# Sink values of two head pairs as two row tiles of the tensor engine, in a fused attention and channel-mix kernel with a written order

## The chip, the cores and the metric

The kernel runs on one core of one Trainium2 chip. The metric is the device time of one execution in microseconds. The engines are named as in the profile: PE (TensorE, with PEld for its weight loads), DVE (VectorE), ACT (ScalarE), POOL (GpSimd) and SP (SyncE, which issues nearly all DMAs). PSUM is the memory into which PE writes its products; it has eight banks.

## The reference

Two layers run one after another. The first is attention over a sliding window of 128 positions with 4 sink positions that every query sees, for 4 batches, 8 heads, 768 positions and a head size of 64. The second is a channel mix with a model width of 512 and a hidden width of 1024.

```python
# attention
scores = scale * np.matmul(q, k.transpose(0, 1, 3, 2))
keep = is_sink | in_window          # pos < 4, or 0 <= query - key < 128
scores = np.where(keep, scores, -1e9)
a = np.exp(scores - max); a = a / (sum(a) + 1e-9)
x = np.matmul(a, v)                 # heads side by side: 512 columns
# channel mix
xk = mu_k * x + (1 - mu_k) * x_prev      # x_prev: the row before
xr = mu_r * x + (1 - mu_r) * x_prev
k = np.maximum(xk @ w_k, 0)
out = sigmoid(xr @ w_r) * (k * k @ w_v)
```

## The kernel before

The work is cut into 12 units, u = 3 * batch + T, of 256 positions each. In the code T is 0, 1 or 2, and g and j count the two blocks of 128 positions in a unit. Four head pairs (c = 0 to 3) make up the eight heads.

`prepare` casts q, k and v of a unit from float32 to bfloat16 (tiles qb, kb, vb) and turns q and k round to qt and kt, with the head's 64 columns of two heads on the 128 partitions. For the early units PE transposes them through a bank, and ACT or DVE copies the bank out (L624). k from unit 4 and q from unit 8 are transposed by a DMA on SP's queue (L603) instead. vb has a column of ones behind each head's 64 columns, so that the sum of the weights comes out as a 65th column. For each batch, `prepare` also makes ksink (the keys of the 4 sinks, by POOL, L655) and vsink (the sinks' values). vsink has the values of every head in rows of its own and zeros elsewhere: hmask keeps, for head h, four rows.

`attend` makes, for units with T > 0, the scores of the sinks (sink_scores, L678: one matmul per head pair, 32 columns of PE each, written to 32 partitions of a bank). ACT takes their exponent into es, which holds all heads: 128 rows and 256 queries. Then come, two head pairs at a time, the scores of the window (scores, L701), which run as two row tiles of 64 partitions, one head each, into the two tiles called sc of two banks each. ACT takes the exponent (L737, e), DVE multiplies the mask in (L751), PE makes the values (values), DVE the reciprocal (L788) and the product x (L791).

In values, one bank takes a head pair: two blocks of queries, two heads, 65 columns. For units with T > 0, each block of queries starts with one sink matmul over all 128 rows (L763), which gives both heads at once, since rows of other head pairs meet zeros of vsink. Then come four matmuls of 65 columns (L775).

`mix` turns x round by PE (L814) and copies it to xt (L823, ACT or DVE). DVE makes the difference td (L841) and the eight mixtures xk and xr (L852). `ffn` makes the hidden layer (L902), the relu (L912 by ACT or L916 by DVE), its square kk (L924, DVE), the gate (L933, with ACT's tanh at L939), the last product (L951, L872) and the output ob (L960, DVE), which SP stores.

Nothing is scheduled at run time. Every operation is put down with `P.op`; its number is its place in that list. ORDER gives each engine's line of operations by number, and each engine works its line through in order. CHOICE says, for some numbers, which engine takes an operation that several could take (casts, copies out of a bank, relus). The planner, `Plan.schedule`, follows the lines with estimated costs, gives out buffers from pools (`take`, held until the last operation that has it under `hold`), and puts filler matmuls (P.fill, L971) into PE's line where it finds PE idle in the first 22 us of its estimate. There are two tiles sc and four single banks, which the sinks' scores, the values, the transposes and all of `ffn` share. `mode` on a PE operation says which partition of the array it uses: 0 is the full array, 1 is row tiles, 2 is the sinks' scores, 4 the transpose of mu.

Of the kernel before, what the change touches and what calls it, by code (L numbers as in the profile page):

```python
# [18 lines left out]
    79: "ACT", 82: "ACT", 83: "ACT", 85: "ACT", 87: "ACT", 89: "DVE", 94: "DVE", 95:  # L19
    "DVE", 97: "DVE", 101: "DVE", 102: "DVE", 128: "DVE", 134: "DVE", 136: "DVE", 137:  # L20
    "DVE", 140: "ACT", 141: "DVE", 150: "DVE", 191: "DVE", 192: "ACT", 193: "ACT", 218:
    "DVE", 265: "DVE", 273: "DVE", 278: "DVE", 305: "DVE", 343: "DVE", 346: "DVE", 348:
    "DVE", 352: "ACT", 354: "DVE", 361: "DVE", 423: "DVE", 429: "ACT", 430: "ACT", 499:
    "DVE", 501: "DVE", 504: "DVE", 507: "DVE", 508: "ACT", 520: "DVE", 586: "ACT", 587:
    "ACT", 654: "DVE", 658: "DVE", 660: "DVE", 663: "DVE", 672: "DVE", 736: "DVE", 738:
    "ACT", 739: "DVE", 744: "DVE", 751: "DVE", 815: "DVE", 816: "ACT", 825: "DVE", 885:
    "DVE", 887: "DVE", 891: "ACT", 892: "ACT", 1003: "DVE",
# [24 lines left out]
        90, 93, 106, 96, 99, 104, 117, 77, 109, 114, 132, 138, 142, 129, 125, 120, 156,  # L52
        135, 158, 149, 184, 190, 169, 236, 208, 209, 212, 213, 220, 221, 161, 166, 172,
        177, 216, 194, 181, 201, 217, 187, 238, 291, 299, 292, 295, 300, 303, 249, 304,
        226, 296, 241, 246, 307, 224, 228, 277, 232, 229, 252, 261, 233, 267, 257, 311,
        264, 284, 270, 312, 319, 344, 309, 315, 330, 316, 349, 367, 375, 368, 376, 322,
        371, 395, 327, 372, 333, 338, 397, 275, 353, 379, 360, 380, 383, 408, 385, 387,
        422, 388, 445, 453, 446, 454, 400, 427, 405, 475, 411, 416, 391, 431, 392, 457,
        438, 458, 449, 473, 486, 450, 463, 526, 530, 527, 531, 500, 538, 461, 505, 539,
        469, 510, 470, 554, 478, 483, 534, 494, 489, 535, 512, 565, 557, 465, 579, 466,  # L60
        542, 519, 544, 562, 550, 584, 573, 551, 588, 546, 568, 632, 602, 547, 603, 606,
        614, 607, 595, 630, 643, 615, 620, 610, 618, 611, 640, 635, 678, 682, 679, 683,
        664, 646, 690, 706, 708, 686, 651, 687, 691, 626, 671, 719, 711, 622, 627, 694,
        623, 761, 757, 765, 758, 762, 766, 722, 696, 741, 727, 716, 775, 785, 702, 750,
        769, 743, 770, 796, 703, 788, 793, 698, 773, 699, 817, 777, 781, 778, 782, 835,
        831, 839, 832, 836, 799, 840, 859, 861, 843, 804, 847, 844, 824, 855, 849, 869,
        864, 872, 856, 907, 915, 908, 851, 916, 852, 880, 875, 911, 893, 912, 919, 900,
        920, 935, 937, 923, 925, 931, 948, 932, 973, 940, 974, 981, 945, 982, 951, 977,
        959, 978, 956, 985, 927, 966, 986, 928, 991, 989, 1001, 1009, 1005, 1002, 1013,
        1006, 1014, 1010, 993, 1021, 997, 994, 998, 1017, 1019, 1022, 1029, 1025, 1030,  # L70
        1026,
    ),
    "DVE": (
        69, 70, 89, 94, 95, 101, 97, 108, 102, 113, 110, 115, 111, 78, 137, 105, 116, 119,
        128, 124, 144, 126, 121, 134, 122, 127, 136, 150, 145, 151, 152, 146, 153, 191,
        147, 160, 148, 165, 80, 81, 154, 171, 141, 176, 162, 163, 167, 173, 168, 178, 174,
        179, 155, 196, 197, 203, 198, 205, 204, 211, 218, 199, 223, 206, 207, 84, 240,
        245, 305, 200, 86, 242, 306, 243, 247, 215, 248, 256, 219, 88, 278, 251, 294, 298,
        279, 230, 253, 302, 254, 234, 258, 259, 280, 265, 343, 286, 348, 281, 282, 287,
        289, 346, 321, 288, 313, 326, 317, 273, 337, 290, 323, 332, 324, 328, 283, 329,  # L80
        334, 339, 335, 340, 370, 354, 276, 374, 355, 361, 358, 362, 382, 356, 378, 364,
        357, 363, 423, 389, 399, 404, 410, 401, 415, 406, 402, 366, 412, 417, 407, 418,
        413, 359, 365, 448, 433, 393, 434, 440, 435, 442, 441, 456, 460, 499, 482, 477,
        504, 452, 529, 501, 488, 507, 436, 493, 511, 437, 471, 479, 480, 484, 444, 485,
        495, 556, 496, 490, 541, 491, 443, 537, 558, 572, 514, 559, 561, 533, 467, 515,
        520, 563, 521, 564, 517, 567, 574, 522, 575, 516, 523, 590, 552, 569, 591, 570,
        518, 525, 548, 524, 654, 634, 593, 639, 597, 660, 599, 658, 592, 598, 605, 645,
        636, 641, 637, 642, 650, 600, 617, 601, 613, 666, 647, 594, 609, 648, 652, 710,
        653, 669, 663, 667, 693, 668, 712, 672, 673, 675, 674, 676, 713, 628, 681, 624,
        670, 736, 721, 715, 726, 723, 724, 677, 685, 728, 729, 689, 760, 717, 742, 718,  # L90
        764, 792, 787, 751, 768, 739, 744, 789, 790, 794, 745, 704, 795, 746, 772, 752,
        748, 803, 747, 754, 753, 755, 700, 819, 779, 783, 798, 820, 749, 822, 834, 800,
        756, 801, 838, 805, 806, 815, 863, 842, 868, 825, 826, 821, 846, 827, 865, 828,
        866, 870, 885, 857, 823, 879, 887, 871, 829, 874, 853, 876, 881, 882, 877, 910,
        830, 918, 895, 898, 914, 902, 896, 922, 903, 939, 904, 944, 897, 933, 950, 941,
        942, 946, 947, 952, 955, 953, 905, 957, 958, 899, 961, 962, 906, 968, 976, 963,
        970, 969, 929, 980, 964, 972, 988, 984, 1003, 965, 1004, 1008, 971, 1012, 1016,
        995, 999, 1023, 1031, 1027,
    ),
    "ACT": (  # L100
        67, 68, 92, 91, 98, 112, 107, 100, 118, 131, 123, 133, 143, 139, 130, 183, 189,
        164, 159, 185, 79, 157, 175, 170, 82, 140, 210, 222, 237, 214, 180, 186, 195, 202,
        182, 192, 188, 244, 239, 293, 83, 301, 193, 255, 227, 250, 85, 297, 308, 87, 225,
        260, 266, 262, 263, 269, 268, 285, 271, 341, 325, 320, 345, 310, 336, 331, 350,
        369, 377, 396, 373, 419, 403, 398, 381, 421, 384, 424, 409, 386, 414, 352, 426,
        447, 455, 428, 481, 476, 432, 497, 439, 429, 502, 459, 451, 474, 487, 464, 528,
        532, 430, 492, 462, 506, 540, 560, 555, 508, 578, 536, 513, 571, 576, 580, 581,
# [188 lines left out]
def kernel(  # L296
# [14 lines left out]
    nc = tc.nc  # L311
    B, H, S, D = q.shape
# [5 lines left out]
    NP = H // 2  # L318
# [7 lines left out]
    P = Plan()  # L326
# [188 lines left out]
    def make_hmask():  # L515
        for a in range(2):
            m = hmask[:, a::2, :]
            keep(m, -4 * a, [[-32, NP], [0, D + 1]], 1, m)
            keep(m, 3 + 4 * a, [[32, NP], [0, D + 1]], -1, m)
# [504 lines left out]
```

## Time and profile before

| what | number |
| --- | --- |
| runs | 170.07, 171.16, 172.91 us; median 171.16 |
| profiled execution | span 172.5 us (the page gives no other time for it) |
| PE busy | 160.6 us (93%) |
| DVE busy | 153.6 us (89%) |
| ACT busy | 129.2 us (75%) |
| POOL busy | 13.4 us (8%) |
| L902 on PE | 384 matmuls, 52.0 us |
| L763 on PE, the sink values | 64 matmuls of 130 columns, 12.4 us |
| L775 on PE, the other values | 352 matmuls of 65 columns, 18.9 us |
| casts of vb on POOL | 3, 2.6 us |
| L971 on PE, fillers | 24 matmuls, 8.8 us |

Busy time is the time in which at least one instruction of the engine runs. Matmuls overlap each other, and their ends are modelled, so that PE's busy time is longer than what its matmuls need one behind another. A line such as L902 is a line of the kernel before. The symbol "<-" behind an idle time names what ended it.

### The profile page before, as it was taken

The page shows a single profiled execution, that of the slowest core. Times are in us where ns is not written, and L with a number is a line of the kernel's source. Part 1 is how long each engine was busy: PE and PEld are TensorE (multiplying, and loading weights), DVE is VectorE, ACT ScalarE, POOL GpSimd, SP SyncE. Part 2 cuts the span into 40 slices and gives each one's busy share as a digit, 9 for nine tenths or more (in the row PEclk, how much of TensorE's full clock was granted, in tenths as well). Part 3 has the DMA queues.
Part 4 walks back from the last instruction along what each step waited for, and adds up shares of the span by engine and source line. Part 5 has one row for each costly group of instructions (what it writes and reads, how often), then busy time and mean ns, then how long its engine had stood idle before and what let it go on. Part 6 is the DMA issues. An engine that isn't in the chain of part 4 may idle for free.

```text
span 172.5 us, 4178 instructions
## 1 busy us (share of the span) xinstructions
PE 160.6 (93%) x1588; PEld 106.3 (62%) x1605; DVE 153.6 (89%) x404; ACT 129.2 (75%) x208; POOL 13.4 (8%) x32
## 2 busy tenths in 40 slices
PE   7986869799999999999999999999999997999992
PEld 2444547675647667777567786756476773777551
DVE  6279895999999999999999999999999999699542
ACT  2488895999898999898979987865838958853320
POOL 7330000000010010050000200120000000000000
PEclk9999678999999999999999999999999999999999
DMA  4999999999156969999679489869969857102033
GB/s 144 243 302 365 291 254 353 380 298 229 26 139 157 287 124 240 197 257 289 163 170 226 96 212 243 159 170 212 240 149 256 213 111 211 61 4 113 11 122 122
DMA packets 81763, 33.82 MB, mean 196 GB/s; under 512 B 63688, under 2 KB 76240, under 8 KB 81744
## 3 DMA queue, kind: packets, MB, share of 16 engines
q1 hardware_dynamic: 81728, 33.56, 78.0%
q8 instruction: 12, 0.20, 0.6%
q14 instruction: 7, 0.06, 0.1%
q10 hardware_dynamic: 16, 0.00, 0.0%
HBM read 24.12 MB, written 6.29 MB: 176 GB/s over the span
## 4 chain that ended last, share of the span: by engine, by line
PE 82%; DVE 10%; DMA 3%; ACT 2%; issue 1%; DVEq 0%; ACTq 0%
PE bank L951 23%; PE bank L902 23%; PE bank L933 12%; PE sc L701 6%; PE bank L775 6%; PE bank L971 4%; PE bank L814 3%; DMA kt<-kb 3%; DVE e L751 2%; PE bank L616 2%; PE bank L763 2%; DVE xk L852 2%; ACT rl L912 1%; ACT e L737 1%; DVE x L791 1%
## 5 line engine op out<-in xcount | busy, mean ns | idle before, releaser
L902 PE MATMUL bank<-xk,wk_sb 128*128 128x256 bf16 x384 | 52.0, 278 | 1.6 <-DVE wk_sb L558 1.3
L737 ACT ACTIVATE e<-sc 128x1024 bf16<-128x1024 f32 (+1 forms) x48 | 44.5, 964 | 4.0 <-PE sc L701 4.0
L951 PE MATMUL bank<-wv_h,kk 128*128 128x512 bf16 x174 | 44.9, 379 | 0.7 <-issue 0.3
L902 PEld LDWEIGHTS <-wk_sb 128*128 128x128 bf16 x384 | 36.1, 100 | 10.2 <-DVE wk_sb L558 1.6
L912 ACT ACTIVATE rl<-bank 128x512 bf16<-128x512 f32 x45 | 26.2, 608 | 12.2 <-PE bank L902 9.6
L751 DVE TENSOR_TENSOR e<-e,mask 128x1024 bf16<-128x1024 bf16 (+1 forms) x48 | 30.0, 637 | 0.7 <-ACT e L737 0.7
L951 PEld LDWEIGHTS <-kk 128*128 128x128 bf16 x184 | 16.7, 98 | 15.8 <-issue 0.7
L933 PE MATMUL bank<-wr_sb,xr 128*128 128x512 bf16 x89 | 23.6, 379 | 0.3
L852 DVE SCALAR_TENSOR_TENSOR xk<-td,mu_all,xt 128x256 bf16<-128x256 bf16 x48 | 22.4, 491 | 0.1
L852 DVE SCALAR_TENSOR_TENSOR xr<-td,mu_all,xt 128x256 bf16<-128x256 bf16 x48 | 22.4, 476 | 0.0
L939 ACT ACTIVATE th<-bank 128x512 f32<-128x512 f32 x24 | 14.7, 618 | 7.8 <-PE bank L933 7.7
L960 DVE SCALAR_TENSOR_TENSOR ob<-th,bank 128x512 f32<-128x512 f32 x23 | 15.6, 680 | 5.6 <-ACT th L939 3.5
L791 DVE TENSOR_TENSOR x<-bank,rec 128x256 bf16<-128x256 f32 x48 | 19.4, 416 | 0.4
L924 DVE TENSOR_TENSOR kk<-rl 128x512 bf16<-128x512 bf16 x48 | 19.4, 415 | 0.1
L775 PE MATMUL bank<-vb,e 128*128 128x65 bf16 x352 | 18.9, 193 | 0.2
L775 PEld LDWEIGHTS <-e 128*128 128x128 bf16 x352 | 16.4, 98 | 3.0 <-DVE e L751 0.7
L701 PE MATMUL sc<-qt,kt 64*128 64x128 bf16 (+1 forms) x256 | 15.0, 246 | 1.7 <-DMA kt<-kb 0.9
L701 PEld LDWEIGHTS <-kt 64*128 64x128 bf16 x256 | 9.4, 97 | 7.9 <-issue 3.4
L933 PEld LDWEIGHTS <-xr 128*128 128x128 bf16 x96 | 8.9, 98 | 8.5 <-issue 0.3
L763 PE MATMUL bank<-vsink,es 128*128 128x130 bf16 x64 | 12.4, 220 | 0.4 <-ACT rl L912 0.3
L823 ACT COPY xt<-bank 128x512 bf16<-128x512 bf16 x15 | 8.8, 586 | 5.3 <-PE bank L814 5.1
L788 DVE RECIPROCAL rec<-bank 128x4 f32<-128x4 f32 x48 | 8.0, 174 | 3.2 <-ACT rl L912 1.8
(67 smaller groups left out, 166.5 us busy)
## 6 DMA issues: line engine op xcount, KB each, us to landing
vs<-in_v_dram SPq DMA_DIRECT2D x24, 256.0 KB, 3.9
out_dram<-ob SPq DMA_DIRECT2D x23, 256.0 KB, 3.2
ks<-in_k_dram SPq DMA_DIRECT2D x18, 256.0 KB, 4.7
qs<-in_q_dram SPq DMA_DIRECT2D x7, 512.0 KB, 9.5
qs<-in_q_dram SPq DMA_DIRECT2D x10, 256.0 KB, 5.4
w<-in_moe_w_k_dram SPq DMA_DIRECT2D x2, 1024.0 KB, 9.2
w<-in_moe_w_v_dram SPq DMA_DIRECT2D x2, 1024.0 KB, 9.9
ks<-in_k_dram SPq DMA_DIRECT2D x3, 512.0 KB, 8.0
```

The lines of the kernel that those rows point to most:

```text
L701: nc.tensor.matmul(out=sc[:, a, o0:o1], lhsT=lhs[rows], rhs=rhs[rows], start=u not in BIAS, stop=True, skip_group_check=u in BIAS)
L737: nc.scalar.activation(out=buf[ek][:, :, lo:], in_=buf[sck][:, :, lo:], func=AF.Exp, scale=scale)
L751: nc.vector.tensor_tensor(out=at, in0=at, in1=m, op=ALU.mult)
L763: nc.tensor.matmul(out=o[:, g, :, :], lhsT=buf["es", u][:, 128 * g:128 * g + 128], rhs=vsink[b % 2][:, 2 * c:2 * c + 2, :], start=True, st ...
L775: nc.tensor.matmul(out=o[:, g, a, :], lhsT=e[:, a, e0:e0 + 128], rhs=rhs, start=(T == 0 and i == 0), stop=(i == len(blocks) - 1), skip_gro ...
L791: P.op("DVE", dve(256), lambda ok=ok, rk=rk, c=c: nc.vector.tensor_tensor(out=buf["x", u][:, :, 128 * c:128 * c + 128].rearrange("p g (a d ...
L852: nc.vector.scalar_tensor_tensor(out=buf[key][:, c0 + i, :], in0=buf[tk][:, i, :], scalar=mu[w][:, c0 + i:c0 + i + 1], in1=xt[:, c0 + i, t ...
L902: nc.tensor.matmul(out=ps[:, i, :], lhsT=wk_sb[:, c, 128 * f:128 * f + 128], rhs=xk[:, c, :], start=(c == 0), stop=(c == NC - 1), skip_gro ...
L912: nc.scalar.activation(out=buf[rk], in_=buf[psk].rearrange("p (i t) -> p i t", i=2), func=AF.Relu)
L924: P.op("DVE", dve(512, 0.52), lambda f2=f2, rk=rk: nc.vector.tensor_tensor(out=buf["kk", u][:, 2 * f2:2 * f2 + 2, :], in0=buf[rk], in1=buf ...
L933: nc.tensor.matmul(out=buf[psk], lhsT=buf["xr", u][:, c, 128 * g:128 * g + 128], rhs=wr_sb[:, c, :], start=(c == 0), stop=(c == NC - 1))
L951: nc.tensor.matmul(out=buf[psk], rhs=wv_h[:, f, :], lhsT=buf["kk", u][:, f, 128 * g:128 * g + 128], start=(f == 0), stop=(f == NF - 1))
```

## The change

The sink rows are laid out anew. Head pair c had the rows from 32c; now it has those from 32 * (c // 2) + 64 * (c % 2). So head pairs 0 and 2 lie in the lower 64 rows, 1 and 3 in the upper. sink_scores writes to these rows, and hmask is made to fit.

The sink matmuls leave values and become an operation of their own, sink_values, once for two head pairs. It takes two banks. For each block of queries it issues two matmuls, one over the lower 64 rows into one bank, one over the upper 64 into the other. The values operations of the two head pairs find their bank taken and add to it. There are 64 such matmuls as before, in 16 operations, and the numbers of all later operations shift.

The tables ORDER and CHOICE are new. In CHOICE POOL has 18 entries, where it had none; POOL's line grows from 13 to 30 operations. It makes 11 casts of qb, 6 of kb, 2 of vb and one of wk_sb; before, it made 3 of vb. On DVE there are fewer casts of kb and qb (6 instead of 16), copies of xt (4 instead of 9), copies of qt (3 instead of 5) and casts of wk_sb (1 instead of 2), and more relus (6 instead of 3), casts of vb (9 instead of 8) and of wv_h (3 instead of 2). On ACT relus go from 45 to 42, casts of wv_h from 2 to 1, of kb from 16 to 14 and of qb from 16 to 11; copies of qt go from 11 to 13 and of xt from 15 to 20. PE's line has 42 fillers instead of 24. SP's line is the same up to the weights, and mixes loads, transposes and stores anew behind them; LOADS and the transposes by DMA stay as they were.

```diff
 CHOICE = {
-    79: "ACT", 82: "ACT", 83: "ACT", 85: "ACT", 87: "ACT", 89: "DVE", 94: "DVE", 95:
+    79: "ACT", 81: "POOL", 82: "ACT", 83: "ACT", 87: "ACT", 91: "DVE", 92: "POOL", 94:
...
 ORDER = {
...
     "POOL": (
-        72, 71, 73, 74, 75, 103, 76, 274, 272, 351, 509, 662, 740,
+        71, 74, 92, 72, 73, 75, 76, 131, 103, 81, 182, 270, 267, 345, 273, 352, 350,
+        278, 425, 430, 432, 356, 512, 436, 591, 517, 670, 825, 752, 903,
     ),
...
     def make_hmask():
         for a in range(2):
-            m = hmask[:, a::2, :]
-            keep(m, -4 * a, [[-32, NP], [0, D + 1]], 1, m)
-            keep(m, 3 + 4 * a, [[32, NP], [0, D + 1]], -1, m)
+            m = hmask[:, a::2, :].rearrange("p (i k) d -> p i k d", k=2)
+            keep(m, -4 * a, [[-32, 2], [-64, 2], [0, D + 1]], 1, m)
+            keep(m, 3 + 4 * a, [[32, 2], [64, 2], [0, D + 1]], -1, m)
...
             def sink_scores():
                 for c in range(NP):
-                    nc.tensor.matmul(out=buf[psk][32 * c:32 * c + 32, 0:256],
+                    r0 = 32 * (c // 2) + 64 * (c % 2)
+                    nc.tensor.matmul(out=buf[psk][r0:r0 + 32, 0:256],
...
+                if T > 0:
+
+                    def sink_values(cs=cs):
+                        for g in range(2):
+                            for r, i in enumerate(cs):
+                                rows = slice(64 * r, 64 * r + 64)
+                                o = buf["o", u, i][:, 130 * g:130 * g + 130]
+                                nc.tensor.matmul(
+                                    out=o.rearrange("p (a d) -> p a d", a=2),
+                                    lhsT=buf["es", u][rows, 128 * g:128 * g + 128],
+                                    rhs=vsink[b % 2][rows, 2 * i:2 * i + 2, :],
+                                    start=(g == 0), stop=False, skip_group_check=True)
+
+                    P.op("PE", 114.0, sink_values, r + 1, lag=PE_LAG, mode=1,
+                         take=[("bank", ("o", u, i)) for i in cs], hold=[("es", u)],
+                         writes=[("os", u, i) for i in cs], reads=[("es", u), ("vsink", b % 2)])
...
                 for g in range(2):
-                    if T > 0:
-                        nc.tensor.matmul(out=o[:, g, :, :],
-                                         lhsT=buf["es", u][:, 128 * g:128 * g + 128],
-                                         rhs=vsink[b % 2][:, 2 * c:2 * c + 2, :],
-                                         start=True, stop=False, skip_group_check=True)
...
-            P.op("PE", 358.0 if T else 180.0, values, r + 1, lag=PE_LAG, take=[("bank", ok)],
-                 hold=[ek, ("vb", u)] + ([("vb", u - 1), ("es", u)] if T else []), writes=[ok],
+            P.op("PE", 232.0 if T else 176.0, values, r + 1, lag=PE_LAG,
+                 take=[] if T else [("bank", ok)],
+                 hold=[ek, ("vb", u)] + ([("vb", u - 1), ok] if T else []), writes=[ok],
```

## The prediction

> **What bounds the kernel now.** I read the page's first two parts first, then the busy time by stretch, because an average hides a start-up and a tail.
>
> ```profile
> PE 160.6 (93%) x1588; PEld 106.3 (62%) x1605; DVE 153.6 (89%) x404; ACT 129.2 (75%) x208; POOL 13.4 (8%) x32
> ...
> PEclk9999678999999999999999999999999999999999
> ```
>
> The digits of PEclk are the granted clock in 40 slices: it sinks once, from 17 to 28 us. By stretch:
>
> ```profile
> 20.70:24.10 3.40, 1.55 (x12) 0.90 (x12) 3.40 (x8) 3.40 (x5) 0.00 (x0) 1.00 1.00 239
> 24.10:27.50 3.40, 3.13 (x15) 2.26 (x16) 2.74 (x6) 1.52 (x3) 0.00 (x0) 0.50 1.00 308
> 30.70:153.40 122.70, 119.74 (x1268) 81.36 (x1282) 119.86 (x315) 102.84 (x167) 7.46 (x9) 1.00 0.82 192
> 153.40:172.50 19.10, 15.85 (x101) 9.64 (x101) 11.55 (x27) 5.44 (x10) 0.00 (x0) 1.00 0.22 83
> ```
>
> The columns of a stretch are its length, then the busy time of PE, PEld, DVE, ACT and POOL, then the granted PE clock. There are three stages. The ramp lasts until 30.7 us, where DVE writes the last x of unit 1. The middle lasts to 153.4, where DVE writes the last x of unit 11. The tail runs to the end. In the middle PE and DVE both show about 98%. DVE's figure is real: its instructions start when the one before lets go, and only 2.8 of 122.7 us are idle. PE's is flattered, since a matmul is counted until its modelled end, long after the next one started (L902: mean 278 ns, but the chain of waits takes 1.75 us for 16, 109 ns each). So I take DVE as the bound of the middle, although the chain puts 82% on PE, and cost the middle on both engines. The tail is PE alone (L902, L951, L933, L872 without a break).
>
> **The change on PE.** In the timeline of PE one sink matmul (L763) starts 0.055 to 0.06 us ahead of the next matmul. The 64 of them take 64 x 0.056 = 3.6 us. As pairs in two row groups and two banks they should behave as the scores' pairs do (L701): twelve of those, six pairs, fit in 0.55 us together with the change of mode. So 32 pairs x 0.056 = 1.8 us remain, and 1.8 us are removed. What speaks against it is what a change of mode costs. In the chain of waits (start, us, what):
>
> ```profile
> 90.19 0.55 PE sc L701 x12
> 90.74 0.54 PE bank L902 x4
> 91.28 0.86 PE bank L951 x4
> 92.15 1.75 PE bank L902 x16
> ```
>
> Four L902 matmuls take 1.75 / 4 = 0.44 us, but 0.54 just behind the scores: leaving the tiled mode costs 0.10. The scores' own columns (two pairs of 256, four of 128) come to 0.45 of their 0.55, so entering costs 0.10 too. Counted along the two written PE orders by the operations' modes, there are 59 changes of mode before and 79 after: 20 x 0.10 = 2.0 us added. PE's account is -1.8 + 2.0 = +0.2 us: nothing is won there. I put it at zero on the path, because PE has cover in the middle. If PE were the bound after all, it would cost 0.2.
>
> The new operation takes two of the four single banks before its first matmul and keeps both until DVE has written the pairs' x. Behind a late bank all of PE's line waits. The trace has only small waits of this kind (L616 on DVE's x, 0.7 us, once), so I bound it by 0 and 1 us and take 0, as the nearest row is one wait in a whole run. The permuted rows in sink_scores and hmask change no count or size.
>
> **The change on DVE and POOL.** The new tables move more than the title says. Counted from the orders, between the last x of unit 1 and the last x of unit 11, DVE loses 6 copies of xt, 5 casts to qb, 2 copies of qt and 1 square, and gains 1 weight cast and 1 relu. DVE overlaps neighbours, so I price by start to start:
>
> ```profile
> 115.03 0.75 DVE L924 TENSOR_TENSOR kk<-rl 128x512 bf16<-128x512 bf16 x2
> 125.93 1.28 DVE L960 SCALAR_TENSOR_TENSOR ob<-th,bank 128x512 f32<-128x512 f32 x2
> 71.41 1.26 DVE L852 SCALAR_TENSOR_TENSOR xk<-td,mu_all,xt 128x256 bf16<-128x256 bf16 x3
> ...
> 47.71 0.61 POOL L638 CAST vb<-vs 128x512 bf16<-128x512 f32 x1
> ...
> 47.26 0.73 DVE L624 COPY qt<-bank 128x512 bf16<-128x512 bf16 x1
> 47.89 0.71 DVE L590 CAST qb<-qs 128x512 bf16<-128x512 f32 x1
> 48.86 0.41 DVE L590 CAST qb<-qs 128x512 bf16<-128x512 f32 x1
> ...
> 61.59 0.81 POOL L638 CAST vb<-vs 128x512 bf16<-128x512 f32 x1 [13.28 <-DMA vs<-in_v_dram]
> 61.45 1.62 DVE L852 SCALAR_TENSOR_TENSOR xk<-td,mu_all,xt 128x256 bf16<-128x256 bf16 x3
> ...
> 73.76 2.44 POOL L655 COPY ksink<-kt 64x16 bf16<-64x16 bf16 x2 [11.36 <-DMA kt<-kb]
> ```
>
> Two squares of about 0.415 each fit in 0.75, so a short operation costs 0.335 us; two L960 of 0.68 in 1.28 make a long one 0.60; a copy of qt takes 0.63 (47.26 to 47.89). Removed: 12 x 0.335 + 2 x 0.63 = 5.3. Added: 2 x 0.60 = 1.2. Net -4.1 us in the middle.
>
> POOL gets the casts. It makes 16 casts in the middle after, 3 before. The three old ones show what one does to DVE: the cast of qb at 47.89 took 0.71 where the next took 0.41 (+0.30); three L852 at 61.45 took 1.62 where three undisturbed ones took 1.26 (+0.36); at 97.07, beside a cast from 96.49 on, two took 1.23 where two others took 0.87 (+0.36). So a cast on POOL holds DVE up for about 0.34 us, as long as DVE itself would need for it. The 13 more cost 13 x 0.34 = +4.4. The bounds are 0, where DVE reads PSUM meanwhile (the ksink copies under the qt copy at 47.26 cost DVE nothing), and a cast's own 0.61, 7.9 us. I take 0.34, the mean of three rows of the same operation.
>
> The Trainium skill ("SBUF — State Buffer", "Who interferes with whom") says that the port pair shared by the two engines is locked for the whole instruction and that the other engine is fully blocked. By that rule the 13 casts would cost up to 7.9 us. The rows show DVE held up for 0.30 to 0.36 under casts of 0.61 to 1.14, so the measurement decides, and the sum does not use the rule.
>
> Middle: -4.1 + 4.4 = +0.3 us, between -4.1 and +3.8. ACT loses about 3 us of work over the run; it is 84% busy in the middle and does not end waits there, so that counts as nothing; were ACT late, DVE's masks would wait.
>
> **The change in the ramp and the tail.** The loads keep their order there. PE's line has 42 filler matmuls instead of 24. Twelve of the new places lie between unit 1's first scores and the first L902. That is where PE is busy for only 1.55 of 3.40 us in the old run, and the clock is 0.50 in the next 3.40: 16 L902 matmuls took 3.44 us there instead of 1.75, and DVE then idled 1.84 us for the first values of unit 1. Fillers there may keep the clock up, worth up to 1.8 us; or they stand ahead of operands that are ready, 12 x 0.216 = 2.6 us late, less what was idle anyway, say +2.0. I take -1.0, nearer the gain, because PE was idle there. In the tail PE's order leaves one more group of four L902 behind the last transpose: +0.4 (0 if the wait for xk covers it).
>
> **Sum.** -1.0 + 0.3 + 0.4 = -0.3 us. Against the profiled execution that is 172.5 - 0.3 = 172.2. That execution lies 1.3 us over the median of the three runs, so the same difference on the median gives 171.16 - 0.3 = 170.9 us. A measurement of this kernel tells about 2%, 3.4 us, from no change.
>
> **Rivals.** First, faster: the new casts mostly fall under DVE operations that read PSUM and cost 0.12 each, 13 x 0.12 = 1.6; the middle wins 2.5, the clock in the ramp the full 1.8, and the tail gives nothing back: 171.16 - 4.3 = 166.9. For it: the reciprocals, x, ob and qt operations are about a third of DVE's time. Against: three casts of three hit operations with SBUF operands.
>
> Second, slower: POOL starves. The copies to ksink at 73.76 took 2.44 us, where a free one takes 0.19, because a gap in DVE's line was awaited. In the new order POOL's line feeds transposes: seven casts (kb of units 4 and 5 twice each, one half of qb in 8, 10 and 11) stand ahead of DMA transposes on SP's queue, with loads, stores and other transposes behind them, and ACT's and DVE's lines wait on scores in turn. A landing late by its own slack already costs: PE waited 0.94 us for kt in unit 11. If a cast is 2 us late and 1 us of it is left over, five units of DVE idleness make 170.9 + 5.0 = 175.9. It decides from the point where DVE's idle time in the middle passes 6 us instead of 2.8. Against it: unit 4's kt was issued by 52.4 and first used at 56.3, some 2 us after it could have landed.
>
> Third, the row tiles don't overlap: es or banks keep the pairs apart. PE then loses 2.0 instead of 0.2, its cover takes most of it, and the time is 170.9 + 1.0 = 171.9. The scores' pairs, which start 3 to 4 ns apart, speak against it.
>
> **How the numbers follow.** Forecast within 2%: 0.46, its own range 168.5 to 173.5. Faster rival 0.20. Slower rival 0.27. No overlap 0.07, which is also within 2%. So faster 0.20, same 0.53, slower 0.27. To leave no more than 2 in 10 outside, the range reaches to the two rivals' times: 166.9 to 175.9.
>
> **What would show it.** Right: L763's successor with 64 rows, starting in pairs a few ns apart; DVE without idle time in the middle, its short operations 0.3 us longer beside POOL's casts; a clock of 1.00 from 24 to 28 us. Wrong: DVE idle for more than 6 us in the middle with SP's transposes waiting for POOL (slower rival), POOL casts beside which DVE keeps its pace (faster rival), sink matmuls 0.056 us apart (third), or a last x of unit 1 later than 32 us (the ramp's sign).

## The result, and the profile after

| kernel | runs, us | median |
| --- | --- | --- |
| before | 170.07, 170.62, 171.16, 172.91 | 170.89 |
| changed | 172.10, 172.30, 172.86, 173.17 | 172.58 |

In this comparison the changed kernel is slower: the ratio is 1.0116, with a 95% interval from 1.0068 to 1.0164. The forecast was 170.9, no change. In all tables the median is of all runs, while ratio and interval leave out runs that lie more than 1.5% above the fastest of their kernel.

Each median here is of four runs. Three larger sets of runs of before, taken later with the experiments, have medians of 172.73 (29 runs), 171.91 (35) and 171.97 (35). The changed kernel was not run beside these; its 172.58 would lie within 0.4% of each. So the 1.7 us rest on four runs of before, three of them quicker than these medians. How much slower the changed kernel is stays open. The firmer finding is that it is not clearly quicker, although its clock did not sink.

Before's own time goes with the granted clock of the execution: from about 170 us at 1.00 to between 171 and 174.6 at 0.98 and less. Of its 111 runs with the experiments only four had a clock of 0.995 or more, and they took 169.79 to 170.27. The changed kernel shows 0.997 to 1.00 in its four runs.

The profiled execution of the changed kernel took 172.3 us and has a span of 170.7. A time thus lies 1.6 us over the span. Its page, the first two parts:

```profile
span 170.7 us, 4240 instructions
...
PE 162.2 (95%) x1623; PEld 103.1 (60%) x1623; DVE 152.5 (89%) x391; ACT 127.5 (75%) x204; POOL 24.3 (14%) x49
...
PEclk9999999999999999999999999999999999999999
```

POOL's busy time went from 13.4 to 24.3, DVE's and ACT's each fell by 1 to 2, and the clock has no dip. By stretch (length, busy time of PE, PEld, DVE, ACT and POOL, then the granted clock, DMA share and GB/s):

```profile
20.70:24.10 3.40, 3.29 (x35) 2.18 (x31) 3.40 (x7) 3.40 (x5) 1.08 (x1) 1.00 0.93 227
24.10:27.50 3.40, 2.55 (x35) 1.75 (x36) 3.40 (x8) 3.02 (x5) 0.61 (x1) 1.00 1.11 322
29.30:151.20 121.90, 120.66 (x1286) 79.34 (x1286) 118.26 (x303) 102.77 (x168) 15.99 (x22) 1.00 0.86 196
151.20:170.70 19.50, 16.18 (x106) 9.99 (x104) 12.18 (x28) 4.78 (x9) 0.00 (x0) 0.99 0.25 94
```

PE is now busy for 3.29 us in the first stretch, where it had 1.55, and the second has a clock of 1.00 instead of 0.50. The last two lines are the middle and the tail, cut again at the last x of unit 1 (29.3) and of unit 11 (151.2). All stage lengths below are cut at these two instructions of DVE. They are taken from the ends of these instructions in the traces, and so is DVE's idle time:

| kernel, one execution each | clock | ramp | middle | tail | DVE idle in the middle |
| --- | --- | --- | --- | --- | --- |
| before, the profile shown | dip | 30.7 | 122.7 | 19.2 | 2.8 |
| before again (first experiment) | dip | 30.4 | 121.5 | 19.2 | 1.8 |
| before with 12 more fillers | no dip | 27.9 | 122.3 | 19.2 | 2.6 |
| changed | no dip | 29.3 | 121.9 | 19.5 | 3.6 |

The first two rows are one kernel, and their middles differ by 1.2 us. A difference of less than that in the middle of a single execution says little.

In the chain of waits of the changed kernel (start, us, what), the sink values show as a piece of their own:

```profile
92.23 0.55 PE sc L708 x12
92.78 0.54 PE bank L921 x4
...
96.36 0.44 PE bank L921 x4
96.80 0.22 PE bank L748 x4
97.02 0.54 PE bank L921 x4
```

L921 (L902 before) takes 0.44 for four, and 0.54 behind the scores as behind the sink values. So leaving the tiled mode costs 0.10. Two pairs at 0.056 are 0.11, and L748 needs 0.22 for them, so entering costs about 0.10 as well. In the trace the two matmuls of a pair start 3 to 4 ns apart. The tiles do overlap, and the changes of mode take the gain.

### The profile page after: what moved, and what is told of

The parts are those of the page before. It is cut to its first block, busy times and chain, and to the rows that moved or that the text cites. A ratio compares the mean times of both kernels' runs of the same rounds, so it can differ in the third digit from the quotient of the medians.

```text
span 170.7 us, 4240 instructions
## 1 busy us (share of the span) xinstructions
PE 162.2 (95%) x1623; PEld 103.1 (60%) x1623; DVE 152.5 (89%) x391; ACT 127.5 (75%) x204; POOL 24.3 (14%) x49
## 4 chain that ended last, share of the span: by engine, by line
PE 77%; DVE 18%; ACT 2%; issue 1%; DVEq 0%
PE bank L970 23%; PE bank L921 20%; PE bank L952 11%; PE bank L793 6%; PE sc L708 5%; DVE e L774 4%; PE bank L990 4%; PE bank L833 3%; DVE xr L871 2%; PE bank L622 2%; DVE x L810 2%; DVE xk L871 2%; DVE kk L943 2%; PE bank L748 2%; DVE vb L644 1%
## 5 line engine op out<-in xcount | busy, mean ns | idle before, releaser
L921 PE MATMUL bank<-xk,wk_sb 128*128 128x256 bf16 x384 | 52.0, 273 | 0.6 <-ACT wk_sb L558 0.4
L970 PE MATMUL bank<-wv_h,kk 128*128 128x512 bf16 x184 | 46.4, 379 | 0.0
L921 PEld LDWEIGHTS <-wk_sb 128*128 128x128 bf16 x384 | 35.3, 98 | 10.3 <-ACT wk_sb L558 1.0
L931 ACT ACTIVATE rl<-bank 128x512 bf16<-128x512 f32 x42 | 25.0, 604 | 13.2 <-PE bank L921 8.9
L774 DVE TENSOR_TENSOR e<-e,mask 128x1024 bf16<-128x1024 bf16 (+1 forms) x48 | 30.6, 649 | 0.0
L943 DVE TENSOR_TENSOR kk<-rl 128x512 bf16<-128x512 bf16 x48 | 20.7, 441 | 0.8 <-ACT rl L931 0.7
L793 PE MATMUL bank<-vb,e 128*128 128x65 bf16 x352 | 16.6, 194 | 1.9 <-DVE e L774 1.3
L842 ACT COPY xt<-bank 128x512 bf16<-128x512 bf16 x20 | 11.9, 593 | 8.6 <-PE bank L833 8.3
L793 PEld LDWEIGHTS <-e 128*128 128x128 bf16 x352 | 13.8, 97 | 6.0 <-DVE e L774 2.3
L708 PE MATMUL sc<-qt,kt 64*128 64x128 bf16 (+1 forms) x256 | 13.9, 238 | 0.3 <-ACT kt L630 0.2
L990 PE MATMUL bank<-warm 128*128 128x512 bf16 x42 | 12.9, 450 | 1.1 <-DVE warm L1006 1.1
```

The lines of the kernel that those rows point to most:

```text
L708: nc.tensor.matmul(out=sc[:, a, o0:o1], lhsT=lhs[rows], rhs=rhs[rows], start=u not in BIAS, stop=True, skip_group_check=u in BIAS)
L774: nc.vector.tensor_tensor(out=at, in0=at, in1=m, op=ALU.mult)
L793: nc.tensor.matmul(out=o[:, g, a, :], lhsT=e[:, a, e0:e0 + 128], rhs=rhs, start=(T == 0 and i == 0), stop=(i == len(blocks) - 1), skip_gro ...
L921: nc.tensor.matmul(out=ps[:, i, :], lhsT=wk_sb[:, c, 128 * f:128 * f + 128], rhs=xk[:, c, :], start=(c == 0), stop=(c == NC - 1), skip_gro ...
L931: nc.scalar.activation(out=buf[rk], in_=buf[psk].rearrange("p (i t) -> p i t", i=2), func=AF.Relu)
L943: P.op("DVE", dve(512, 0.52), lambda f2=f2, rk=rk: nc.vector.tensor_tensor(out=buf["kk", u][:, 2 * f2:2 * f2 + 2, :], in0=buf[rk], in1=buf ...
```

## The experiments

Ratios are against runs of the kernel before that were taken together with the experiment. The changes of mode are counted from the traces.

### Before again, and the two halves of the change

The first kernel is before, unchanged. The second has the new code for the sinks in before's orders: each sink_values is put just ahead of the first values of its two head pairs.

```diff
 # tiles in the old orders
-CHOICE, ORDER = (those of the changed kernel)
+CHOICE, ORDER = (those of before, renumbered, with each sink_values
+                 ahead of the first values of its pairs in PE's line)
```

The third has the new orders and the old sink matmuls.

```diff
 # new orders, old sinks
-CHOICE, ORDER = (those of before)
+CHOICE, ORDER = (those of the changed kernel, renumbered, without sink_values)
```

> The kernel before, unchanged, for a second profile. Theory 1 (the yardstick): the profiled execution of before was not a typical one; its PE clock sat at 0.50 in two stretches of the ramp, which cost about 1.7 us and more behind it. Then this profile shows a span of 168.5 to 169.5 us, a mean clock of 0.99 or more, and the last x of unit 1 by 29.5 us. Rival 1: the dip of the clock belongs to this kernel's ramp; then the span is 171 to 173 us with a clock of 0.98, and the times lie above the span as they do for the changed kernel.

> Only the row tiles: the changed sink values (two banks, two row tiles) in the orders and choices of before, each new operation put just ahead of the first values of its two head pairs. Its PE order has 85 changes of mode, before had 59. Theory 2 (the tiles cost more than they save): 26 x 0.10 - 1.8 = +0.8 us on PE, and up to 1 us of waits for two banks, together +0.8 to +1.8 us over before. Rival 2 (PE has cover, the loss is in the new orders): within 0.4 us of before. If the tiles do what they are for: 1 us or more below before.

> Only the new orders and choices: the kernel before with its own sink matmuls inside values, but with the changed kernel's lines and engines. 61 changes of mode, 42 fillers. Theory 2 (the tiles cost): 0 to +0.7 us against before, as 18 changes of mode fewer than in the changed kernel give 1.8 us back and the full sink matmuls take 1.8. Rival 2 (the orders cost, by casts on POOL that hold DVE up, or by the fillers): +1.0 to +2.0 us against before.

| kernel | median us | ratio, 95% interval |
| --- | --- | --- |
| before again | 172.14 (170.0 to 174.11) | 1.0034 [0.9987, 1.0081] |
| tiles in the old orders | 176.12 | 1.0244 [1.0190, 1.0299] |
| new orders, old sinks | 174.00 | 1.0059 [1.0005, 1.0112] |

Before against itself gives the grain of the measurement. Its runs here went from 169.8 (clock 1.00) to 174.6, and its second profile shows the dip again, as the rival in the first expectation had it.

The tiles alone cost most. There are 85 changes of mode in that kernel, 26 more than before, which is 2.6 us at 0.10; the pairs save 1.8 of it. Most of the rest is waits. In its middle, 3.9 us longer than that of before again, the timeline of PE shows the line standing still (start, us, what, and in brackets the idle time before and what ended it):

```profile
107.20 1.89 PE L956 MATMUL bank<-wv_h,kk 128*128 128x512 bf16 x8 [0.58 <-DVE xt L828]
...
114.62 0.27 PE L734 MATMUL bank<-vsink,es 64*128 64x130 bf16 x3 [0.57 <-ACT rl L917]
```

L734 is the sink matmul there. Of a group of four the first starts at 113.82, in the first bank; the second needs the other bank and waits until 114.62 for ACT to read it out. Its waits list in the same stretch (engine, tile, line, what it waited for: us, times, longest) shows DVE standing still in turn:

```profile
DVE ob L965 <- PE bank L956: 1.0, 1, 1.0
...
DVE rec L793 <- PE bank L779: 0.9, 1, 0.9
```

In the prediction, the hold of two banks was bounded by 0 and 1 us. In the old orders the waits come to more than that, and in the changed kernel PE never stands idle for more than 0.02 us ahead of a sink matmul. So the orders belong to the tiles, and the two halves can't be added up: 2.4% and 0.6% alone, 1.2% together. The new orders alone cost about 1 us, and their interval, 0.1 to 1.9 us, covers both cases of their expectation.

### The casts on POOL

Is it the casts on POOL that cost the time? All 20 are given back, 15 to ACT and 5 to DVE.

```diff
 # changed, without POOL's casts
-    92: "POOL", 131: "POOL", 267: "POOL", ... (20 casts)
+    92: "ACT", 131: "ACT", 267: "ACT", ...    (15 on ACT, 5 on DVE, moved in ORDER)
```

> The changed kernel with its casts on POOL (6 of kb, 11 of qb, 2 of vb, 1 of wk_sb) given back to the engines that made them before (15 to ACT, 5 to DVE), each at its place in time. Theory 3 (POOL's casts hold DVE up by 0.3 us each, and that is the loss): DVE gets 13 to 16 x 0.3 = 4 to 5 us back, pays 5 x 0.34 = 1.7 for its own, so 1.5 to 3 us below the changed kernel. Rival 3 (they pay, because ACT needs the relief): 15 x 0.62 = 9 us more on ACT make it 0 to 3 us slower than the changed kernel.

It took 172.65 us, ratio 1.0031 [0.9995, 1.0067]. That is the time of the changed kernel (172.58), which was taken in another set of runs. The ramp is 1.5 us shorter (27.8), but the middle is 0.8 and the tail 1.0 longer, with ACT busy for 134.1 us instead of 127.5. The casts as a whole are not the loss. But the ramp gained by losing them, and this led to the question which cast it was.

What a cast does to DVE shows in the timeline of the changed kernel:

```profile
51.37 0.61 POOL L593 CAST kb<-ks 128x512 bf16<-128x512 f32 x1 [3.48 <-DMA ks<-in_k_dram]
54.31 0.61 POOL L593 CAST kb<-ks 128x512 bf16<-128x512 f32 x1 [2.33 <-DMA ks<-in_k_dram]
...
51.28 0.68 DVE L979 SCALAR_TENSOR_TENSOR ob<-th,bank 128x512 f32<-128x512 f32 x1
...
54.38 0.96 DVE L774 TENSOR_TENSOR e<-e,mask 128x768 bf16<-128x768 bf16 x1
...
10.81 0.54 DVE L774 TENSOR_TENSOR e<-e,mask 128x768 bf16<-128x768 bf16 x1
```

The first cast falls beside an ob, which reads a bank, and costs nothing: 0.68 is what ob takes elsewhere. The second falls beside a mask with both operands in SBUF: 0.96 instead of 0.54. Measured like this against the median of each kind, the 16 casts of the middle held DVE up by 2.5 us together, 0.16 each. Six DVE instructions were held up by 0.27 to 0.42, one of them beside two casts. Beside the other nine casts it was 0.11 or less.

### The clock

Before is given 12 more fillers (the edit asks for 14, and 12 find a free bank), in the places where the changed kernel has its own between unit 1's scores and the first hidden layer.

```diff
 # before with fillers
+MORE = {129: 3, 135: 2, 236: 3, 212: 6}
...
+            for _ in range(MORE.get(i, 0)):
+                some = [b for b in free["bank"] if b[0] <= t]
+                if some:
+                    order.append(("fill", self.pools["bank"][min(some)[1]]))
             order.append(i)
```

The other way round, the changed kernel loses the 12 fillers of its two such places.

```diff
 # changed, without 12 fillers
+NONE = [170, 210]
-            if o["engine"] == "PE" and self.fill:
+            if o["engine"] == "PE" and self.fill and i not in NONE:
```

> The kernel before with 12 more filler matmuls in the ramp: 3 and 2 ahead of the transposes of unit 1's k, up to 3 ahead of unit 2's sink scores, up to 6 behind the first eight L902. Nothing else is changed. Theory 4 (the ramp's clock is what spreads the times of before, and fillers hold it): every run has a clock of 0.995 or more, the times lie within 1 us of each other at about 169.9, 1.5 to 3 us below the median of before, and the last x of unit 1 is written by 28.5 us. Rival 4 (the dips are noise that fillers don't touch, or fillers delay as much as they save): clocks of 0.97 to 1.00 and a median of 171 to 173.

> The changed kernel without the 12 fillers between unit 1's first scores and the first L902. Theory 4 (they hold the clock): the clock falls to 0.5 for 3.4 us or more behind 20 us in most runs, and the time rises by 1 to 2 us with a spread of 2 us or more. Rival 4 (they stand ahead of operands that are ready): the time falls by 0.5 to 2 us at a clock of 1.00.

Before with fillers took 170.83 us, ratio 0.9932 [0.9900, 0.9964], with a clock of 0.997 to 1.00 in all 12 runs, which lie within 170.47 and 171.98. The clock by stretch, of before again:

```profile
17.00:20.50 3.50, 3.37 (x36) 2.51 (x37) 2.75 (x7) 2.77 (x5) 0.00 (x0) 0.54 1.11 350
20.50:24.00 3.50, 1.55 (x12) 0.89 (x11) 3.50 (x8) 3.50 (x6) 0.00 (x0) 0.94 0.87 197
24.00:27.50 3.50, 3.22 (x20) 2.39 (x21) 2.76 (x6) 1.53 (x3) 0.00 (x0) 0.57 1.09 303
```

And of before with fillers:

```profile
17.00:20.50 3.50, 2.41 (x29) 1.53 (x30) 3.40 (x9) 3.48 (x5) 0.00 (x0) 1.00 1.10 357
20.50:24.00 3.50, 3.49 (x27) 2.21 (x25) 3.50 (x8) 3.50 (x6) 0.00 (x0) 1.00 0.92 184
24.00:27.50 3.50, 3.17 (x58) 2.94 (x56) 3.10 (x12) 2.93 (x7) 0.00 (x0) 1.00 1.13 279
```

PE is kept busy from 20.5 to 24, the clock is 1.00 in all three stretches, and the ramp is 27.9 us instead of 30.4. So the dip costs about 2.5 us between these two executions. On the median it is 1.1 us: 170.83 against 171.91 for the 35 runs of before taken with it, most of which have a clock between 0.97 and 0.99. A ramp without a dip should be compared with the 27.9. The changed kernel's is 1.4 us longer than that.

The clock does not explain every spread. Below, the kernel with ones first ran from 169.57 to 174.54 at clocks of 0.996 to 1.00, and the new orders with the old sinks ran from 171.7 to 175.82 at 0.994 to 1.00. What spreads those is open.

Taking fillers out of the changed kernel gave 172.18, ratio 1.0020 [0.9985, 1.0055]. The clock dipped for one stretch (0.50 from 21.75 to 25.16 in its profile), and the ramp was as long as with them (29.4). So taking them out changed little, though the changed kernel itself (172.58) was taken in another set. Neither expectation had the size.

### The first cast of q

The ramp's 1.4 us were looked for from the front. The timeline of the changed kernel, DVE, POOL, PE, then ACT:

```profile
2.63 0.17 DVE L470 MEMSET ones<- 128x128 bf16 x1
...
2.87 0.29 POOL L484 TENSOR_SCALAR_AFFINE_SELECT ident<-ones 128x128 bf16<-128x128 bf16 x1 [2.35 <-DVE ones L470]
...
3.72 1.83 POOL L484 TENSOR_SCALAR_AFFINE_SELECT hmask<-hmask 128x260 bf16<-128x260 bf16 x4
5.50 0.61 POOL L596 CAST qb<-qs 128x512 bf16<-128x512 f32 x1
...
4.94 1.79 PE L990 MATMUL bank<-warm 128*128 128x512 bf16 x4
6.57 0.39 PE L622 MATMUL bank<-ident,qb 128*128 128x128 bf16 x4
...
8.15 0.81 ACT L760 ACTIVATE e<-sc 128x768 bf16<-128x768 f32 x1 [1.20 <-PE sc L708]
```

In the new order DVE's line puts the memsets that are wanted late (fill_later, 1.6 us of them) ahead of the one that makes ones. POOL's first instruction waits for ones until 2.87; in before it starts at 1.28. CHOICE gives the first cast of q to POOL, behind hmask, at 5.50. There is no idle time before the cast: q had landed, POOL was late. Unit 0's q is turned round only behind this cast, and all scores wait for it. In this execution something else is added: the cast ends at 6.11, but four fillers (L990) hold PE until q's transposes start at 6.57. In the kernel with full rows (below), whose start is the same, the four take 1.15 us instead of 1.79, and the transposes follow the cast's end at once:

```profile
4.94 1.15 PE L990 MATMUL bank<-warm 128*128 128x512 bf16 x4
6.15 0.40 PE L622 MATMUL bank<-ident,qb 128*128 128x128 bf16 x4
```

So of a late first exponent some 0.4 us belong to this execution and not to the cast.

The cast is late against its operand, and not against before. There ACT makes it at 4.6 to 4.7, but seven fillers stand ahead of the transposes, and the first exponent starts later than 8.15: at 8.81 and 8.57 in its two profiles, and in the one with 12 more fillers at 8.25:

```profile
8.25 1.50 ACT L744 ACTIVATE e<-sc 128x768 bf16<-128x768 f32 x2
```

So in these profiles the change does not make the start later; it leaves a wait in it that can be taken out. Three edits try this, each by itself: the casts of q of units 0 and 1 to ACT; that of unit 0 alone to ACT; and, with all casts left on POOL, the two memset groups swapped back. In each the planner also puts two fillers instead of four between the transposes of k and of q.

```diff
 # first q casts on ACT: 92 and 131 (unit 0 alone: 92)
-    92: "POOL", ... 131: "POOL",
+    92: "ACT", ... 131: "ACT",    (and moved from POOL's to ACT's line)
```

```diff
 # ones first
 "DVE":
-    70, 69, 91, ...
+    69, 70, 91, ...
```

> The changed kernel with two casts of its POOL line, the first halves of q in units 0 and 1, back on ACT. Theory 5 (the ramp is late because POOL reaches the first cast of q only behind hmask, 0.8 us later than ACT): the first exponent starts at 7.4 instead of 8.2 us, the last x of unit 1 at 28.3 to 28.8 instead of 29.6, and the time falls by 0.8 to 1.4 us, to 171.2 to 171.8. Rival 5 (the ramp's head start is lost before the end, as it was without any casts on POOL): 172.3 to 172.9.

> The changed kernel with one cast of POOL back on ACT, the first half of q in unit 0. Theory 5 (this cast stands first in the chain of the whole ramp, and POOL gets to it 0.8 us late): most of what both casts gave, 0.8 to 1.7 us, so 170.9 to 171.8, the first exponent at 7.4 us. Rival 5b (it is the second cast, of unit 1, behind a wait for q's load): 172 to 172.9.

> The changed kernel with the first two entries of DVE's line swapped, so that the memset of ones comes first, as before. All casts of POOL stay. Theory 7 (POOL is late, not slow: its first instruction waits until 2.87 us for DVE's memset of ones, which stands behind 2 us of other memsets): POOL starts at about 1.3 us, makes the first cast of q at 4.7 instead of 5.5, and the time falls by 0.8 to 1.7 us, to 170.9 to 171.8. Rival 7 (a cast on POOL is itself slower for those behind it): 172.3 to 172.9.

| kernel | median us | ratio, 95% interval | ramp | first exponent starts |
| --- | --- | --- | --- | --- |
| changed | 172.58 | 1.0116 [1.0068, 1.0164] | 29.3 | 8.15 |
| casts of units 0 and 1 on ACT | 170.40 | 0.9913 [0.9879, 0.9947] | 27.7 | 7.41 |
| cast of unit 0 on ACT | 170.64 | 0.9922 [0.9885, 0.9960] | 27.8 | 7.52 |
| ones first | 170.60 | 0.9932 [0.9895, 0.9970] | 27.6 | 7.26 |

Any of the three is 1.9 to 2.2 us below the changed kernel, which was taken in another set of runs. The two kernels with the late cast that were taken together with the first edit, full rows and the one without 12 fillers, took 171.95 and 172.18, and it took 170.40. So 1.5 to 2.2 us go with the late cast. The timeline with ones first, POOL, ACT and DVE:

```profile
1.28 0.29 POOL L469 TENSOR_SCALAR_AFFINE_SELECT ident<-ones 128x128 bf16<-128x128 bf16 x1 [0.77 <-DVE ones L455]
...
4.79 0.61 POOL L581 CAST qb<-qs 128x512 bf16<-128x512 f32 x1 [0.82 <-DMA qs<-in_q_dram]
...
7.26 0.81 ACT L745 ACTIVATE e<-sc 128x768 bf16<-128x768 f32 x1 [0.20 <-PE sc L693]
...
22.34 1.04 POOL L549 CAST wk_sb<-w 128x1024 bf16<-128x1024 f32 x1 [9.47 <-DMA w<-in_moe_w_k_dram]
...
22.50 0.68 DVE L920 TENSOR_SCALAR rl<-bank 128x512 bf16<-128x512 f32 x1
```

POOL now waits for q's landing, and casts as fast as before (0.61). It was late, not slow. The first exponent starts 0.89 us earlier. How the 0.7 us by which the cast comes earlier (4.79 instead of 5.50) become 1.7 at the end of the ramp shows in the changed kernel's timeline, POOL and then DVE:

```profile
11.18 0.63 POOL L596 CAST qb<-qs 128x512 bf16<-128x512 f32 x1 [3.03 <-DMA qs<-in_q_dram]
...
21.07 1.08 POOL L564 CAST wk_sb<-w 128x1024 bf16<-128x1024 f32 x1 [8.44 <-DMA w<-in_moe_w_k_dram]
...
11.27 0.83 DVE L644 CAST vb<-vs 128x512 bf16<-128x512 f32 x1
...
12.49 0.42 DVE L644 CAST vb<-vs 128x512 bf16<-128x512 f32 x1
...
21.17 1.26 DVE L871 SCALAR_TENSOR_TENSOR xr<-td,mu_all,xt 128x256 bf16<-128x256 bf16 x1
...
22.95 0.47 DVE L871 SCALAR_TENSOR_TENSOR xr<-td,mu_all,xt 128x256 bf16<-128x256 bf16 x1
```

Here POOL's cast of unit 1's q meets a cast of DVE (0.83 instead of 0.42), and its cast of wk_sb meets a mixture (1.26 instead of 0.47). That is 0.41 and 0.79 more. With ones first, DVE is ahead when these loads land; the cast of wk_sb falls beside a relu from a bank, which keeps its 0.68. It is the same in the other profiles: in four of the five with the late cast the cast of wk_sb costs DVE 0.78, in the four with an early cast 0.15 at most. Matched instruction by instruction, DVE's lateness against the kernel with ones first is 0.89 at 7.3 us, 1.31 at 12.3, 2.07 at 22.7, and 1.69 at the last x of unit 1, part of it won back at waits.

### What the tiles themselves are worth

The changed kernel with full rows again (rows 32c, all 128 rows in each sink matmul, in the new operation and orders, 61 changes of mode instead of 79); the changed kernel with its sink matmuls issued twice over; and full rows together with the early casts on ACT.

```diff
 # full rows
-                                rows = slice(64 * r, 64 * r + 64)
+                                rows = slice(0, 128)
...
-                    P.op("PE", 114.0, sink_values, r + 1, lag=PE_LAG, mode=1,
+                    P.op("PE", 114.0, sink_values, r + 1, lag=PE_LAG, mode=0,
 # sinks twice
-                        for g in range(2):
+                        for g in (0, 1, 0, 1):
```

> The changed kernel with its operation for sink values and its orders, but each sink matmul over all 128 rows as before (rows of other head pairs meet zeros), no row tiles: 61 changes of mode instead of 79. By the account on PE: 1.8 us more for the matmuls, 18 x 0.10 = 1.8 us less for the changes of mode, so 172.6 within 0.4. If the row tiles run together and changes of mode are cheap where they are: 1.0 to 1.8 us slower. If the pairs did not overlap: 1.8 us faster.

> The changed kernel with every group of sink matmuls issued twice (the second pass overwrites the first, the result is the same): 32 more pairs of row tiles, 32 x 0.056 = 1.8 us more work on PE, spread over the 16 operations, no more changes of mode. Theory 6 (in the middle PE's line sets the time as much as DVE's): +1.2 to +1.8 us, 173.8 to 174.4. Rival 6, the prediction's reading (DVE is the bound and PE has cover): within 0.5 us of the changed kernel, 172.1 to 173.1.

> Both first casts of q on ACT, and the sink matmuls over full rows in their own operation (no row tiles): the two edits that took time off the changed kernel, together. If they add up: 170.4 - 0.6 = 169.8. If the full rows were within noise: 170.4 within 0.4.

| kernel | median us | ratio, 95% interval |
| --- | --- | --- |
| changed, full rows | 171.95 | 0.9966 [0.9922, 1.0009] |
| changed, sinks twice | 173.81 | 1.0057 [0.9998, 1.0116] |
| full rows, first casts of q on ACT | 170.35 | 0.9913 [0.9878, 0.9948] |

Full rows are 0.6 us quicker than the changed kernel's median, less than its runs spread, and with the early casts they give the same time as the tiles do (170.35 and 170.40). The tiles win nothing. Full rows alone came out 0.25 below the range that was expected by the account on PE (172.6 within 0.4). The doubled sinks settle little: 1.8 us more of PE work made the middle 0.4 us longer in the profile and the median 1.2 higher, and that profile is of one of its quickest runs (171.97 of 171.57 to 174.97).

## Why the prediction was wrong

**The step that failed: the ramp term.** It was -1.0, with bounds of -1.8 and +2.0. The prediction said of the ramp that the loads keep their order there, and named the fillers as the one thing that could cost time. It put the start of POOL's and DVE's lines at nothing and gave no reason. A cast had been put there behind masks that wait for a memset that had been moved. Three edits that bring this cast forward take the time from 172.58 to between 170.40 and 170.64, and the ramp from 29.3 to between 27.6 and 27.8. Beside kernels with the late cast that were taken together with them, it is 1.5 to 1.8 us. So a term of +1.5 to +2.2 us was missing.

The clock's part of the term was about right: twelve fillers alone took before's median down by 1.1 us (171.91 to 170.83). With the cast early the kernel is 0.7 to 0.9% below before, somewhat more than the forecast of -0.3 us.

What this does not show is why the new order needs its early start. From the first exponent to the last x of unit 1 the changed kernel takes 21.2 us, the three kernels with an early cast 20.2 to 20.4, and before with fillers, whose first exponent comes later, 19.7. About 0.8 of the difference thus goes with the late cast and its two collisions. Why the new order takes 0.6 us and more beyond before's was not traced.

**From the profile to the median: luck.** The prediction says "the same difference on the median gives 171.16 - 0.3 = 170.9 us". It set a span (172.5) against times and found it 1.3 us over the median. With 1.6 between span and time, that execution was one of about 174.1, 2.9 over the median and above each of the three runs shown. Against this execution the changed kernel's span is 1.8 us shorter and not 0.3: ramp -1.4 (forecast -1.0), middle -0.8 (+0.3), tail +0.3 (+0.4). Against before again (span 171.0) it is 0.3 shorter: ramp -1.1, middle +0.4, tail +0.3. That this fits the forecast is luck, as the two executions of before differ by 1.5 us. Against before with fillers (span 169.4) it is 1.3 us longer: ramp +1.4, middle -0.5, tail +0.3. Against before's few runs at a clock of 1.00 (169.8 to 170.3) the time is 2.3 to 2.8 us longer.

The Trainium skill ("TensorE: Matmul & The Clock Gate", Part 1) has windows of some 3.4 us, after an idle one of which the clock is halved, and says that they run free, so that the point of change differs from run to run. The rows agree in part: before's dip was 0.50 for 3.40 us, and the changed kernel's stretches, with PE busier, are at 1.00. But the stretch ahead of the dip was not idle; PE was busy for 1.55 of 3.40.

**DVE and POOL in the middle: the sum within the noise, the terms not right.** Thirteen more casts were to cost 13 x 0.34 = 4.4 us. All 16 cost 2.5, and before's three 1.0, so that the 13 more cost about 1.5. Beside instructions that read a bank they cost next to nothing, and nine of the 16 cost 0.11 or less; the three old rows all happened to meet operands in SBUF. DVE got lighter: it is busy for 118.26 us in the middle, where before had 119.86. Yet the middle (121.9) did not get shorter by more than the 1.2 us by which two executions of before differ (122.7 and 121.5), and DVE's idle time rose from between 1.8 and 2.8 us to 3.6. Its waits in the middle, in the waits list (us, times, longest):

```profile
DVE rec L807 <- PE bank L793: 1.6, 6, 0.4
```

The list of before again has no row of this kind; its longest is 0.7 us for ACT's tanh. So DVE is not alone the bound in the middle, as the prediction took it. That what it was spared went into waits for PE fits these rows, but no run shows it by itself.

The Trainium skill's rule on the shared ports ("SBUF — State Buffer", "Who interferes with whom"), which the prediction set aside, has the other engine fully blocked, and exempts DVE instructions with no more than one input in SBUF unless they run in a 2-port mode. The rows go with it further than the prediction did: up to 0.79 of a cast's 1.08 and 0.41 of 0.63, and nothing beside ob or relu. That no cast costs its whole length stays as measured.

**PE: right, as far as the runs tell.** -1.8 + 2.0 = +0.2 was the account of the tiles. The chain shows 0.10 for each change of mode, and full rows give the same time within the spread.

**The rivals.** The third (no overlap) did not come: pairs start 3 to 4 ns apart. The first (cheap casts, a full gain of the clock) was near in both: the casts cost 0.16 each, where it had 0.12, and the clock gave 1.1 on the median, where it had 1.8. Its 166.9 did not come, as the late cast took back what the clock gave and the middle did not get shorter. The second (POOL starves) showed in part. A cast of vb in the changed kernel's timeline:

```profile
74.15 3.16 POOL L644 CAST vb<-vs 128x512 bf16<-128x512 f32 x1 [7.19 <-DMA vs<-in_v_dram]
...
74.28 1.28 DVE L774 TENSOR_TENSOR e<-e,mask 128x1024 bf16<-128x1024 bf16 x2
75.48 0.42 DVE L644 CAST vb<-vs 128x512 bf16<-128x512 f32 x1
75.82 0.42 DVE L943 TENSOR_TENSOR kk<-rl 128x512 bf16<-128x512 bf16 x1
76.15 0.68 DVE L774 TENSOR_TENSOR e<-e,mask 128x1024 bf16<-128x1024 bf16 x1
```

POOL took 3.16 us for what takes 0.61 free, with DVE's instructions on SBUF operands at their usual length beside it. But DVE's idle time stayed below the 6 us from which the rival was to decide, and without POOL's casts the time was the same (172.65).

**The signs.** Of the four alarms one rang in part: beside nine of the 16 POOL casts DVE kept its pace, the sign of the faster rival. The others did not, the last x of unit 1 (29.3, alarm at 32) among them. That limit was set from a dipped execution; before with fillers, without a dip, is at 27.9. Of the signs of being right, the pairs a few ns apart and the clock of 1.00 came, and a DVE without idle time did not.

## What to carry to other kernels

In a start-up, follow every engine's line from its first instruction, the memsets too: a swap of two of them was worth more here than the whole change of the matmuls. Before a difference is carried from a profiled execution to a median, bring both to one measure (span against span, time against time) and ask whether the execution has something, here a dip of the clock, that most others have less of. Four runs of a kernel whose time spreads by 5 us are few: three quick ones of before may be a good part of the difference here. Row tiles pay only when what they save between two changes of mode is more than the two changes cost (here 0.11 against 0.20).

## What the runs showed of the hardware

A change of mode of PE's array costs 0.10 us each way. A POOL cast of 0.61 us to 1.08 us held up DVE instructions with SBUF operands by up to 0.42 and 0.79 us, and left those that read a bank alone. The other way round, a cast of POOL that takes 0.61 us free took 3.16 beside DVE instructions on SBUF operands. Twelve filler matmuls of 512 columns were enough to hold the clock at 0.997 to 1.00 in 12 runs of 12, where runs of the same kernel without them went down to 0.96.

Of the kernels here five have intervals wholly below before: the three with the first cast of q early (170.40, 170.64 and 170.60), the one with full rows and early casts (170.35), and before with 12 more fillers (170.83).
